# Random-feature attention and a routed expert layer: head reordered, routing cut up, weight pieces regrouped, row buffers freed earlier

## The chip, the cores and the metric

The kernel runs on one core of one Trainium2 chip. The time of a run is the device time of one execution in microseconds (us). The engines are TensorE (PE, its weight loads PEld), VectorE (DVE), ScalarE (ACT), GpSimd (POOL) and SyncE (SP), which only issues transfers. Transfers issued by GpSimd are here the weight pieces, the gathers and the scatters.

## The reference

```python
def _attn_ref(q, k, v, omega):            # q, k, v (8, 8, 576, 64), omega (128, 64)
    def phi(x):
        proj = np.einsum('bhsd,md->bhsm', x, omega)
        return np.concatenate([np.cos(proj), np.sin(proj)], axis=-1) / np.sqrt(m)
    q_p, k_p = (phi(q), phi(k))
    kv = np.einsum('bhsm,bhsd->bhmd', k_p, v)
    z = np.sum(k_p, axis=2)
    num = np.einsum('bhsm,bhmd->bhsd', q_p, kv)
    den = np.einsum('bhsm,bhm->bhs', q_p, z)
    ...
    return num / den
...
x = attn_out.transpose(0, 2, 1, 3).reshape(4608, 512)
def _moe_ref(x, expert_emb, tau, w1, w2): # 8 experts, w1 (8, 512, 1024), w2 (8, 1024, 512)
    xn = x / (np.linalg.norm(x, axis=-1, keepdims=True) + 1e-06)
    en = expert_emb / (np.linalg.norm(expert_emb, axis=-1, keepdims=True) + 1e-06)
    logits = xn @ en.T / tau
    expert_idx = np.argmax(logits, axis=1)
    ...                                   # gate_w: softmax probability of the chosen expert
    for e in range(8):
        mask = expert_idx == e
        h = np.maximum(x[mask] @ w1[e], 0.0)
        out[mask] = gate_w[mask, None] * (h @ w2[e])
```

## The kernel before

The work has three stages. The **head** sets up constants and computes the key side of steps 0 and 1. The **loop** `for n in range(1, NS + 1)` has 32 steps (NS = 32), one for each batch and pair of heads; it is a software pipeline, so step n holds the query side of pair n, the numerator of pair n-1, the key side of pair n+1 and the key projection of pair n+2. The **blocks** `for j in range(NMAIN)` are 40 blocks of 128 tokens, each of one expert; three more stand under a condition.

In a loop step TensorE runs `proj_q` (L245), `num` (L358), `proj_k` (L232), `turns` (L207, L209), `kv_products` (L309) and `kv_turn` (L326 on the products, L333 on the key sums). VectorE runs `frac` (L272) and `fold` (L278), which bring projections into the range of the sine, `split_q` (L201), `kv_copy` (L319) and `norm`. ScalarE rounds (`whole_turns`, L266) and takes sines (`wave`, L284), two for keys and two for queries. GpSimd adds the features over the tokens: `zsum(n, half)` is four additions (L296 to L299) after the sine of that half, and their result `zs` is read by L333. It also issues the weights of the experts as 32 pieces of 512 KB (`emit_weight_piece`, L92 and L98, converted from float32 to float16 on the way): three in the head and one at the end of each step up to 29. On even steps it adds the router's logits (`sums`, L391 to L394).

`set_up_tables`, `set_up_emb`, `set_up_unit` and `set_up_turn` in the head make the router's constants and the matrix `rmat` (L510, GpSimd; L522, VectorE) that `kv_turn` multiplies by. The first three key tiles are copied from PSUM by VectorE (`copy_k`, L218 and L219, tile `w_sb`), later ones by ScalarE.

Routing runs on VectorE in small instructions. `choose_a` (L655 to L658) brings logits together, `choose_b` (L664 to L667) finds the best expert, `choose_c` (L671) marks it, `scan` (L687) counts. `route_first(n)` puts these at steps 9, 10, 17, 18 and 25 to 29, and the placing of the tokens of the first half (`rank`, `places`, `block_hot`, `row_hot`, `rows_of`, `block_experts`) at 18 to 26. In program order a piece of routing stands ahead of `fold(n + 1, "k")` and `frac(n, "q")` on VectorE. `early_second` places the first three quarters of all tokens at steps 30 and 31, and `route_second(j)` the rest in the blocks j = 0 to 7.

In a block, GpSimd issues `gather(j)` (L849, 128 rows of 521 words to a row buffer of `xin_all`), `cast` (L882, to float16), `power` (L893, the norm) and the scatter of the result (L1004). ScalarE squares the rows (L886). VectorE's `score` (L899 to L906) and `weigh` (L916 to L922) work on nine more words of each row, eight logits and the token's number, which `score` reads from the row buffer. TensorE transposes the rows (`turn_x`, L928), and runs `hidden` (L969) and `result` (L991). Gather j+5 uses the buffer of block j or of a block shortly after it, so it waits until the readers of that buffer are through.

The order on every engine is the order in which the program is written; each engine runs its own list, held up only by semaphores.

Of the kernel before, what the change touches and what calls it, by code (L numbers as in the profile page):

```python
# [28 lines left out]
def kernel(  # L29
# [56 lines left out]
    W1BASE, W2BASE = 18046, 83328  # L86

# [50 lines left out]
    with tc.tile_pool(name="psA", bufs=1, space=PSUM) as psA, tc.tile_pool(  # L138
# [150 lines left out]
        def zsum(n, half):  # L289
# [6 lines left out]
            nc.gpsimd.tensor_tensor(zt, t[:, 0:3], t[:, 3:6], ALU.add)  # L296
            nc.gpsimd.tensor_tensor(zt, zt, t[:, 6:9], ALU.add)
# [136 lines left out]
        nc.gpsimd.memset(rmat[64:P, :, :, 0], 0.0)  # L434
        nc.vector.memset(zmask, 0.0)
# [4 lines left out]
        def set_up_tables():  # L440
# [5 lines left out]
            nc.gpsimd.iota(tmpi[:, 0:P], pattern=[[1, P]], base=0, channel_multiplier=0)  # L446
            nc.gpsimd.memset(tri, 0.0)
# [97 lines left out]
        set_up_tables()  # L545
        warm(10)
# [6 lines left out]
        copy_k(0)  # L553
        set_up_norms()
        for b in range(2):
# [8 lines left out]
        turns(1)  # L564
        set_up_emb()
# [172 lines left out]
        def places_a(rk, s0, s1, ar):  # L738
            ns = s1 - s0
            d = [ar.take(ns) for _ in range(4)]  # L740
            pick(d[0], rk[:, :, 0:ns].rearrange("p e s -> p s e"), s0, s1, ar)
            whole(d[1], d[0], -0.49609375)
# [3 lines left out]
            return d  # L746

        def places_b(d, s0, s1, ar):
            shp = [P, s1 - s0, E]
            pick(d[2], bc(sm[:, B1], shp, 1), s0, s1, ar)  # L750
            nc.vector.tensor_tensor(p2["at"][:, s0:s1], d[1], d[2], ALU.add)
            pick(d[3], bc(sm[:, LIM], shp, 1), s0, s1, ar)
            nc.vector.tensor_tensor(p2["ge"][:, s0:s1], d[0], d[3], ALU.is_ge)
# [11 lines left out]
        def places2(w, ge, ns, ar):  # L765
            dest = ar.take(ns)
            lo = ar.take(ns, FP16)
            blk = ar.take(ns, FP16)
# [4 lines left out]
            nc.vector.tensor_reduce(dest.unsqueeze(2), w, axis=AX.X, op=ALU.add)  # L773
            whole(blk, dest, -0.49609375, ar.take(ns))
# [120 lines left out]
        def score(j):  # L895
            t = xin.pop(j).bitcast(FP32)
            s = gsc[:, j % 4]
            rn, mx, sh = s[:, 1:2], s[:, 2:3], s[:, 4 : 4 + E]
            nc.vector.tensor_tensor(  # L899
                ptk[:, j : j + 1], t[:, D + E : D + NG].bitcast(I32), bad[:, j : j + 1], ALU.max  # L900
            )
            lg = t[:, D : D + E]
# [3 lines left out]
            nc.vector.tensor_scalar(sh, lg, mx, rn, ALU.subtract, ALU.mult)  # L906
# [5 lines left out]
        def weigh(j):  # L912
            s = gsc[:, j % 4]
            z = s[:, 3:4]
            sh, dn = s[:, 4 : 4 + E], s[:, 4 + E : 4 + 2 * E]
# [418 lines left out]
```

## Time and profile before

| what | value |
|---|---|
| median of 3 runs | 496.03 us (491.79 to 497.04) |
| the profiled execution | 495.86 us |
| its span, first to last instruction | 494.1 us |
| mean granted clock of TensorE | 0.965 of 2.4 GHz |
| busy, share of the span | PE 93%, POOL 79%, DVE 73%, ACT 69% |

The profiled execution is 0.17 us below the median, and 1.8 us of it lie outside the span. The first loop step begins at 31.90 us, the first `result` of the blocks at 331.53 us, and the last matrix product ends at 484.95 us. A granted clock of 1.00 is 2.4 GHz, 0.50 is 1.2 GHz; a share between them is a mean over the stretch.

### The profile page before, as it was taken

How to read it: one execution, taken by the hardware profiler on the slowest of the kernel's cores; microseconds unless marked ns; L12 is line 12 of the kernel's file. 1: busy time of each engine (PE TensorE's matmuls, PEld its weight loads, DVE VectorE, ACT ScalarE, POOL GpSimd, SP SyncE). 2: the span in 40 equal slices, each digit the busy share in tenths (PEclk: the TensorE clock that was granted, in tenths of full speed). 3: DMA queues.
4: the chain of work that ended last, by engine and by line, in shares of the span. 5: the costliest groups of instructions: out<-in, count | busy, mean ns of one | idle time of the engine just before them, and what ended most of it. 6: DMA issues, size and time to landing. Idle time of an engine off the chain costs nothing. (4 is left out here: it accounts for less than half of the span.)

```text
span 494.1 us, 19396 instructions
## 1 busy us (share of the span) xinstructions
PE 459.2 (93%) x7963; PEld 380.7 (77%) x7963; DVE 360.4 (73%) x969; ACT 338.8 (69%) x475; POOL 388.3 (79%) x519
## 2 busy tenths in 40 slices
PE   8699999989999998998999999699899999999992
PEld 7588887879888887887887888486577777777771
DVE  3747776787766789987889878777876666666671
ACT  2668887978788877887787888357565555555551
POOL 7968898786888787877787888837688888888861
PEclk9779999998999999998999999899899999999997
DMA  6666988887978869889679895506344443443420
GB/s 196 131 146 140 202 169 211 192 172 161 201 166 189 202 141 214 168 199 198 137 187 175 177 222 95 131 24 165 102 131 132 129 133 121 128 134 125 126 74 34
DMA packets 58633, 75.10 MB, mean 152 GB/s; under 512 B 10918, under 2 KB 37542, under 8 KB 58544
## 3 DMA queue, kind: packets, MB, share of 16 engines
q0 software_dynamic: 19200, 35.83, 35.0%
q1 hardware_dynamic: 39040, 37.93, 28.8%
q8 instruction: 65, 1.06, 0.9%
q14 instruction: 24, 0.20, 0.1%
q10 hardware_dynamic: 304, 0.08, 0.1%
HBM read 72.62 MB, written 20.09 MB: 188 GB/s over the span
## 5 line engine op out<-in xcount | busy, mean ns | idle before, releaser
L969 PEld LDWEIGHTS <-w_sb 128*128 x1280 | 74.7, 98 | 10.1 <-issue 1.5
L358 PE MATMUL ps<-kv,siq 128*64 128x73 f32 x1152 | 79.1, 234 | 0.0
L969 PE MATMUL ps<-qr,w_sb 128*128 128x128 f16 x1280 | 78.0, 219 | 0.4 <-DVE qr L197 0.4
L358 PE MATMUL ps<-kv,coq 128*64 128x73 f32 x1152 | 77.3, 231 | 1.0 <-ACT coq L284 1.0
L991 PE MATMUL ps<-w_sb,coq 128*128 x320 | 76.9, 384 | 0.3 <-issue 0.3
L358 PEld LDWEIGHTS ps<-kv,siq 128*64 128x64 f32 x1152 | 60.5, 139 | 12.2 <-issue 11.7
L296 POOL TENSOR_TENSOR zt<-sik 128x384 f32<-128x384 f32 x32 | 43.4, 1355 | 33.6 <-ACT sik L284 33.4
L358 PEld LDWEIGHTS ps<-kv,coq 128*64 128x64 f32 x1152 | 61.4, 141 | 1.2 <-ACT coq L284 1.2
L849 POOL DMA_INDIRECT xin_all<-rf_x,prm x40 | 42.5, 1063 | 23.7 <-issue 13.5
L272 DVE SCALAR_TENSOR_TENSOR cok<-cok,ps 128x1024 f32<-128x1024 f32 (+2 forms) x61 | 46.3, 758 | 16.0 <-ACT cok L266 14.5
L991 PEld LDWEIGHTS <-coq 128*128 128x128 f16 x320 | 30.6, 99 | 29.9 <-issue 2.1
L272 DVE SCALAR_TENSOR_TENSOR coq<-coq,ps 128x1152 f32<-128x1152 f32 x32 | 43.3, 1352 | 12.3 <-ACT coq L266 10.5
L284 ACT ACTIVATE siq<-coq 128x1152 f32<-128x1152 f32 x32 | 37.3, 1164 | 15.2 <-DVE coq L272 9.0
L245 PE MATMUL ps<-qr,omT 32*128 32x288 f32 x512 | 44.4, 432 | 2.9 <-issue 1.7
L886 ACT ACTIVATE qT<-xin_all 128x512 f16<-128x512 f32 x40 | 25.2, 629 | 31.5 <-DMA xin_all<-rf_x,prm 31.5
L284 ACT ACTIVATE cok<-cok,pio 128x1152 f32<-128x1152 f32 x31 | 38.8, 1253 | 10.0 <-DVE cok L278 9.9
L232 PE MATMUL ps<-omT,kT 64*128 64x128 f32 x522 | 41.0, 284 | 4.0 <-DVE coq L272 4.0
L296 POOL TENSOR_TENSOR zt<-cok 128x384 f32<-128x384 f32 x32 | 39.6, 1237 | 5.5 <-ACT cok L284 3.4
L278 DVE TENSOR_SCALAR cok<-cok 128x1152 int32<-128x1152 int32 x31 | 26.5, 854 | 22.0 <-ACT sik L284 21.9
L284 ACT ACTIVATE coq<-coq,pio 128x1152 f32<-128x1152 f32 x32 | 40.2, 1256 | 2.0 <-DVE coq L278 1.9
L232 PEld LDWEIGHTS ps<-omT,kT 64*128 64x128 f32 x522 | 34.8, 187 | 7.0 <-DVE coq L272 4.5
L266 ACT ACTIVATE cok<-ps 128x1152 f32<-128x1152 f32 x31 | 35.0, 1128 | 6.5 <-PE ps L207 4.4
(207 smaller groups left out, 1233.4 us busy)
## 6 DMA issues: line engine op xcount, KB each, us to landing
w_sb<-in_moe_w_dram POOLq DMA_DIRECT2D x32, 512.0 KB, 7.2
qr<-in_q_dram SPq DMA_DIRECT2D x64, 144.0 KB, 5.5
rf_x<-xb SPq DMA_DIRECT2D x32, 288.0 KB, 5.7
kr<-in_k_dram SPq DMA_DIRECT2D x58, 144.0 KB, 4.0
v<-in_v_dram SPq DMA_DIRECT2D x32, 144.0 KB, 4.4
xin_all<-in_v_dram SPq DMA_DIRECT2D x30, 144.0 KB, 8.4
w_sb<-in_k_dram SPq DMA_DIRECT2D x6, 144.0 KB, 2.9
xin_all<-rf_x,prm POOLq DMA_INDIRECT x40, 3.5
```

The lines of the kernel that those rows point to most:

```text
L232: nc.tensor.matmul(kreg[:, KS[c] * P : KS[c] * P + P], lhsT=t[r0 : r0 + 64, j * P : j * P + P], rhs=omT2[r0 : r0 + 64], start=True, stop=True,
L245: nc.tensor.matmul(qreg[:, g // 2, QW * (g % 2) : QW * (g % 2) + QW], lhsT=omT4[r0 : r0 + 32, b], rhs=t[r0 : r0 + 32].rearrange("p (c b j) ...
L266: nc.scalar.activation(dst, src, AF.Copy, bias=CMAGIC, scale=1.0)
L272: nc.vector.scalar_tensor_tensor(out=dst, in0=dst, scalar=CMAGIC, in1=src, op0=ALU.subtract, op1=ALU.subtract)
L278: nc.vector.tensor_scalar(t, t, 0x7FFFFFFF, None, ALU.bitwise_and)
L284: nc.scalar.activation(st[n][which + nm], t, AF.Sin, bias=pio2 if which == "co" else 0.0, scale=-TWO_PI * SINSC,)
L296: nc.gpsimd.tensor_tensor(zt, t[:, 0:3], t[:, 3:6], ALU.add)
L358: nc.tensor.matmul(nm[r0 : r0 + 64, c], lhsT=ph[:, 2 * QW * hh + 64 * c : 2 * QW * hh + 64 * c + 64], rhs=d["kv"][:, hh, half], start=(hal ...
L849: ins = nc.gpsimd.indirect_dma_start(out=t, out_offset=None, in_=x_rows[:], in_offset=bass.IndirectOffsetOnAxis(ap=prm[:, j : j + 1], axis=0),
L886: nc.scalar.activation(late("qT", j % 2, D), xin[j].bitcast(FP32)[:, 0:D], AF.Square, accum_out=gsc[:, j % 4, 0:1],)
L969: nc.tensor.matmul(h_ps[:, f * P : f * P + P], lhsT=weights(k), rhs=d["xT"][:, c * P : c * P + P], start=(c == 0), stop=(c == 3),)
L991: nc.tensor.matmul(y_ps, lhsT=d["hT"][:, c * P : c * P + P], rhs=weights(NW1 + c), start=(c == 0), stop=(c == NW2 - 1),)
```

## The change

Five things change. The pieces of weights are issued two at the very start (ahead of the constant tables on GpSimd), three between the key sums of the head, and then only in odd steps: one between the first and the second addition of `zsum(n + 1, 0)` and one at the step's end. In the head the key side of step 1 comes earlier, `frac(1, "k")` stands ahead of `turns(2)`, and the set-up of the router is spread between. The routing of the first half is spread over more steps in smaller parts, and the third quarter's `choose` moves to steps 27 to 29. In the last steps the gathers 0, 1 and 2 stand at the ends of steps 28, 29 and 30, cast 0 stands ahead of gather 2, and `hot(0)`, `hot(1)` and `hot(2)` (the one-hot tables of places) move into step 32 and into block 0. Finally `cast` gets a second GpSimd instruction, which copies the nine extra words of a row to `gsc`; `score` reads them there, so that the row buffer is read by GpSimd and ScalarE alone.

```diff
+
+    pieces = list(range(4 * E - 4)) + [4 * E - 2, 4 * E - 1, 4 * E - 4, 4 * E - 3]
+
+    def next_piece():
+        if pieces:
+            emit_weight_piece(pieces.pop(0))
...
             nc.gpsimd.tensor_tensor(zt, t[:, 0:3], t[:, 3:6], ALU.add)
+            if between is not None:
+                between()
             nc.gpsimd.tensor_tensor(zt, zt, t[:, 6:9], ALU.add)
             nc.gpsimd.tensor_tensor(z, zt[:, 0], zt[:, 1], ALU.add)
             nc.gpsimd.tensor_tensor(z, z, zt[:, 2], ALU.add)
...
         nc.gpsimd.memset(rmat[64:P, :, :, 0], 0.0)
+        next_piece()
+        next_piece()
...
         proj_q(0)
         load_q(3)
-        turn_emb()
-        set_up_unit()
         for s in cuts:
             part(0, "si", s)
+        copy_k(1)
+        proj_k(1)
+        turn_emb()
+        whole_turns(0, "q")
+        for s in cuts:
             part(0, "fold", s)
-        for s in cuts:
             part(0, "co", s)
         zsum(0, 0)
-        emit_weight_piece(0)
-        copy_k(1)
-        split_q(1)
-        set_up_turn()
-        whole_turns(0, "q")
-        proj_k(1)
+        next_piece()
+        set_up_unit()
+        frac(0, "q")
         whole_turns(1, "k")
-        frac(0, "q")
         kv_products(0)
         zsum(0, 1)
-        emit_weight_piece(1)
+        next_piece()
+        split_q(1)
         wave(0, "si", "q")
+        frac(1, "k", slice(0, P))
+        frac(1, "k", rest)
         turns(2)
-        frac(1, "k")
         wave(1, "si", "k")
+        zsum(1, 0)
+        next_piece()
+        fold(0, "q")
         kv_copy(0)
-        fold(0, "q")
         wave(0, "co", "q")
         load_v(2)
         copy_k(2)
+        set_up_turn()
         fold(1, "k")
         wave(1, "co", "k")
-        zsum(1, 0)
-        emit_weight_piece(2)
+        zsum(1, 1)
         proj_k(2)
-        kv_turn(0)
         turns(3)
         load_k(4)
-        zsum(1, 1)
         whole_turns(2, "k")
         copy_k(3)
+        frac(2, "k", rest)
         kv_products(1)
-        frac(2, "k", rest)
         kv_copy(1)
         frac(2, "k", slice(0, P))
+        kv_turn(0)
...
         def cast(j):
             x16 = late("v", j % 2, D)
             nc.gpsimd.tensor_copy(x16, xin[j].bitcast(FP32)[:, 0:D])
+            nc.gpsimd.tensor_copy(
+                gsc.bitcast(I32)[:, j % 4, 4 : 4 + NG], xin[j][:, D : D + NG]
+            )
             mo[j] = {"x16": x16}
 
         def square(j):
+            t = xin.pop(j).bitcast(FP32)
             nc.scalar.activation(
-                late("qT", j % 2, D), xin[j].bitcast(FP32)[:, 0:D], AF.Square,
-                accum_out=gsc[:, j % 4, 0:1],
+                late("qT", j % 2, D), t[:, 0:D], AF.Square, accum_out=gsc[:, j % 4, 0:1]
             )
 
         def power(j):
@@ -893,17 +917,15 @@
             nc.gpsimd.tensor_tensor(s[:, 1:2], s[:, 0:1], half1, ALU.pow)
 
         def score(j):
-            t = xin.pop(j).bitcast(FP32)
             s = gsc[:, j % 4]
-            rn, mx, sh = s[:, 1:2], s[:, 2:3], s[:, 4 : 4 + E]
+            rn, mx, lg = s[:, 1:2], s[:, 2:3], s[:, 4 : 4 + E]
             nc.vector.tensor_tensor(
-                ptk[:, j : j + 1], t[:, D + E : D + NG].bitcast(I32), bad[:, j : j + 1], ALU.max
-            )
-            lg = t[:, D : D + E]
+                ptk[:, j : j + 1], s.bitcast(I32)[:, 4 + E : 4 + NG], bad[:, j : j + 1], ALU.max
+            )
             nc.vector.tensor_reduce(mx, lg, axis=AX.X, op=ALU.max)
             nc.vector.tensor_scalar(rn, rn, 1e-6, None, ALU.add)
             nc.vector.reciprocal(rn, rn)
-            nc.vector.tensor_scalar(sh, lg, mx, rn, ALU.subtract, ALU.mult)
+            nc.vector.tensor_scalar(lg, lg, mx, rn, ALU.subtract, ALU.mult)
 
         def tanh(j):
             sh = gsc[:, j % 4, 4 : 4 + E]
...
         def route_first(n):
-            if n == 9:
-                choose_a(0)
-                choose_b(0)
-            elif n == 10:
-                choose_c(0)
-                store_logits(0)
-            elif n == 17:
-                choose_a(1)
-                choose_b(1)
-            elif n == 18:
-                choose_c(1)
-                store_logits(1)
-                scan()
-            elif n == 19:
+            if n in (9, 17, 27):
+                choose_a((n - 9) // 8)
+            elif n in (10, 18, 28):
+                choose_b((n - 9) // 8)
+                store_logits((n - 9) // 8)
+            elif n in (11, 19, 29):
+                choose_c((n - 9) // 8)
+                if n > 11:
+                    scan()
+            elif n == 20:
                 r1["rk"] = ar1.take((S1 + 1) * E).rearrange("p (e s) -> p e s", e=E)
                 nc.vector.tensor_copy(r1["rk"], r1["ps"])
-            elif n == 20:
+            elif n == 21:
                 starts1b()
                 r1["wg"] = places(r1["rk"], S1, ar1)
-            elif n == 21:
-                r1["blk"], r1["lo"] = places2(*r1["wg"], S1, ar1)
             elif n == 22:
+                r1["at"] = places2(*r1["wg"], S1, ar1)
+            elif n == 23:
+                r1["blk"], r1["lo"] = places3(r1["at"], S1, ar1)
                 r1["rr"] = block_hot(r1["blk"], S1, 0, K1, ar1)
-            elif n == 23:
+            elif n == 24:
                 row_hot(oh1[:, 0:SG], r1["lo"][:, 0:SG])
-            elif n == 24:
+            elif n == 25:
                 row_hot(oh1[:, SG:S1], r1["lo"][:, SG:S1])
-            elif n == 25:
+            elif n == 26:
                 rows_of(r1["inv"], 0, K1, ar1)
-                choose_a(GRP1)
-            elif n == 26:
                 block_experts(0, K1, False, ar1)
-            elif n == 27:
-                choose_b(GRP1)
-                store_logits(GRP1)
-            elif n == 28:
-                choose_c(GRP1)
-            elif n == 29:
-                scan()
+            elif n == 30:
+                ar = p2["ar"] = Arena(pa.tile([P, 5 * P], FP32, tag="kT", name="ar", bufs=1))
+                p2["lo"] = ar.take(NSLOT, FP16)
+                p2["at"] = ar.take(NSLOT)
+                p2["ge"] = ar.take(NSLOT)
+                p2["d"] = places_a(p2["rk"], 0, S3, ar)
...
@@ -1122,15 +1125,14 @@
                     load_q(n + 3)
             if n == NS:
                 hidden(0, "act")
+                turn_x(1, "dve")
+                hot(0)
                 cast(2)
-                square(2)
-                power(1)
...
-                zsum(n + 1, 0)
+                zsum(n + 1, 0, next_piece if n % 2 else None)
...
-                turn_x(0, "dve")
+                square(0)
...
+            if last:
+                power(0)
+                turn_x(0, "act")
...
-            if n + 2 < NS:
-                emit_weight_piece(n + 2)
+            if n == 29:
+                p2["rk"] = rank(0, S3, ROUTE)
+            if n % 2:
+                next_piece()
             if n == NS - 4:
                 gather(0)
             elif n == NS - 3:
                 gather(1)
+            elif n == NS - 2:
+                places_b(p2["d"], 0, S3, p2["ar"])
+                p2["oh"] = [row_tile(), row_tile()]
+                cast(0)
                 gather(2)
-            elif n == NS - 2:
-                cast(0)
-                square(0)
+            elif last:
+                places_c(p2["d"], 0, S3, p2["ar"])
+                score(0)
                 cast(1)
-            elif last:
-                power(0)
-                score(0)
                 square(1)
                 gather(3)
-                turn_x(1, "dve")
-                early_second(n)
             elif n == NS:
+                power(1)
+                square(2)
                 gather(4)
                 tanh(0)
                 weigh(0)
+                hot(1)
+                score(1)
```

VectorE in step 9 of the loop, before: `choose_a` and `choose_b` stand between `split_q` and the key `fold`.

```order
L201 STREAM_TRANSPOSE qr<-qr 128x576
L655 COPY lsq<-la 64x9x8
L656 COPY lsq<-la 64x9x8
L657 TENSOR_TENSOR lsq<-lsq,la 64x9x8
L658 TENSOR_TENSOR lsq<-lsq,la 64x9x8
L664 TENSOR_REDUCE lmax<-lsq 128x9
L665 TENSOR_TENSOR sel<-lsq,lmax 128x72
L666 TENSOR_TENSOR sel<-sel,pref 128x72
L667 TENSOR_REDUCE pm<-sel 128x9
L278 TENSOR_SCALAR cok<-cok 128x1152
L272 SCALAR_TENSOR_TENSOR coq<-coq,ps 128x1152
```

VectorE in step 9, after: only `choose_a` stands there.

```order
L207 STREAM_TRANSPOSE qr<-qr 128x576
L670 COPY lsq<-la 64x9x8
L671 COPY lsq<-la 64x9x8
L672 TENSOR_TENSOR lsq<-lsq,la 64x9x8
L673 TENSOR_TENSOR lsq<-lsq,la 64x9x8
L284 TENSOR_SCALAR cok<-cok 128x1152
L278 SCALAR_TENSOR_TENSOR coq<-coq,ps 128x1152
```

VectorE in step 10, after.

```order
L207 STREAM_TRANSPOSE qr<-qr 128x576
L679 TENSOR_REDUCE lmax<-lsq 128x9
L680 TENSOR_TENSOR sel<-lsq,lmax 128x72
L681 TENSOR_TENSOR sel<-sel,pref 128x72
L682 TENSOR_REDUCE pm<-sel 128x9
L284 TENSOR_SCALAR cok<-cok 128x1152
L278 SCALAR_TENSOR_TENSOR coq<-coq,ps 128x1152
```

`choose_b` has moved by one step, to the same place between `split_q` and `fold`; `choose_c` follows in step 11.

GpSimd at the end of step 29, before: the last weight piece and two gathers, then the key sums of step 31.

```order
L98 DMA w_sb<-in_moe_w_dram 128x4x512
L849 DMA xin_all<-rf_x,prm 128x521 x2
L296 TENSOR_TENSOR zt<-sik 128x384
L297 TENSOR_TENSOR zt<-zt,sik 128x384
L298 TENSOR_TENSOR zs<-zt 128x128
L299 TENSOR_TENSOR zs<-zs,zt 128x128
```

GpSimd at the same place, after.

```order
L870 DMA xin_all<-rf_x,prm 128x521
L302 TENSOR_TENSOR zt<-sik 128x384
L305 TENSOR_TENSOR zt<-zt,sik 128x384
L306 TENSOR_TENSOR zs<-zt 128x128
L307 TENSOR_TENSOR zs<-zs,zt 128x128
```

The weight piece is gone from here (the last one went at step 27), and gather 2 has moved behind the key sums of step 31.

GpSimd in the blocks, before, one round and the scatter that starts the next.

```order
L1004 DMA out_dram<-siq,ptk 4608x512
L849 DMA xin_all<-rf_x,prm 128x521
L893 TENSOR_TENSOR gsc<-gsc,half_77 128x1
L882 CAST v<-xin_all 128x512
L1004 DMA out_dram<-sik,ptk 4608x512
L849 DMA xin_all<-rf_x,prm 128x521
```

GpSimd in the blocks, after.

```order
L1026 DMA out_dram<-siq,ptk 4608x512
L870 DMA xin_all<-rf_x,prm 128x521
L917 TENSOR_TENSOR gsc<-gsc,half_77 128x1
L903 CAST v<-xin_all 128x512
L904 COPY gsc<-xin_all 128x9
L1026 DMA out_dram<-sik,ptk 4608x512
L870 DMA xin_all<-rf_x,prm 128x521
```

One copy of nine words (L904) has come in behind each cast; the order of the rest is the same. In the program before, such a gather waits for VectorE and for GpSimd; now it waits for GpSimd alone, and the copy waits for VectorE's work on an earlier block's `gsc`.

## Rows read from the trace of the kernel before

**Rows 1.** Windows: engine busy us (instructions), granted clock share, DMA share, GB/s.

```profile
50.00:60.00 10.00, 10.00 (x221) 8.57 (x215) 7.27 (x13) 8.90 (x11) 8.28 (x11) 1.00 0.94 203
310.00:320.00 10.00, 5.10 (x48) 3.90 (x46) 7.18 (x15) 3.63 (x6) 9.42 (x13) 0.82 0.57 139
320.00:330.00 10.00, 8.97 (x187) 8.55 (x184) 7.26 (x16) 4.71 (x9) 2.66 (x3) 0.84 0.04 8
425.00:470.00 45.00, 45.00 (x534) 33.67 (x532) 29.85 (x157) 25.31 (x61) 38.87 (x49) 1.00 0.40 127
```

**Rows 2.** Timeline of TensorE at L245: start, length; steps 2, 9, 10, 11, 29.

```profile
40.84 0.53 PE L245 MATMUL ps<-qr,omT 32*128 32x288 f32 x4
...
103.78 0.53 PE L245 MATMUL ps<-qr,omT 32*128 32x288 f32 x4
...
115.94 0.53 PE L245 MATMUL ps<-qr,omT 32*128 32x288 f32 x4
...
124.69 0.53 PE L245 MATMUL ps<-qr,omT 32*128 32x288 f32 x4
...
295.69 0.53 PE L245 MATMUL ps<-qr,omT 32*128 32x288 f32 x4
```

**Rows 3.** Timeline of VectorE in step 9.

```profile
104.26 0.22 DVE L655 COPY lsq<-la 64x72 f32<-64x72 f32 x1
...
107.70 0.23 DVE L667 TENSOR_REDUCE pm<-sel 128x9 bf16<-128x72 bf16 x1
108.69 1.34 DVE L272 SCALAR_TENSOR_TENSOR coq<-coq,ps 128x1152 f32<-128x1152 f32 x1
```

**Rows 4.** Waits of TensorE, 42 to 300 us: total, times, longest.

```profile
PE ps L232 <- DVE coq L272: 4.0, 3, 1.5
PE ps L245 <- issue: 1.7, 3, 0.7
```

**Rows 5.** Waits of TensorE, 300 to 335 us.

```profile
PE ps L333 <- POOL zs L299: 4.6, 2, 3.8
```

**Rows 6.** Timeline of GpSimd at the end of the loop.

```profile
308.90 1.11 POOL L849 DMA_INDIRECT xin_all<-rf_x,prm  x1 [0.30 <-issue]
310.04 1.02 POOL L296 TENSOR_TENSOR zt<-sik 128x384 f32<-128x384 f32 x1
```

**Rows 7.** Waits of GpSimd, 331 to 370 us.

```profile
POOL xin_all L849 <- DVE gsc L921: 4.6, 3, 3.0
```

**Rows 8.** Waits of TensorE, 331 to 370 us.

```profile
PE ps L928 <- POOL v L882: 2.6, 2, 2.2
```

**Rows 9.** Timeline of GpSimd over one block of the experts.

```profile
426.19 1.04 POOL L849 DMA_INDIRECT xin_all<-rf_x,prm  x1 [0.30 <-DMA xin_all<-rf_x,prm]
427.25 0.58 POOL L893 TENSOR_TENSOR gsc<-gsc,half 128x1 f32<-128x1 f32 x1
427.80 0.61 POOL L882 CAST v<-xin_all 128x512 f16<-128x512 f32 x1
428.58 1.06 POOL L1004 DMA_INDIRECT out_dram<-siq,ptk  x1 [0.18 <-issue]
429.95 1.03 POOL L849 DMA_INDIRECT xin_all<-rf_x,prm  x1 [0.30 <-DMA xin_all<-rf_x,prm]
```

**Rows 10.** Groups of GpSimd by line and shape: busy, mean ns.

```profile
L98 POOL DMA_DIRECT2D w_sb<-in_moe_w_dram x16 | 12.3, 767 | 0.0
...
L510 POOL COPY rmat<-ident 64x128 f32<-64x128 f32 x8 | 2.4, 332 | 0.1
...
L459 POOL IOTA lsq<- 32x16 int32 x4 | 0.7, 163 | 0.1
```

**Rows 11.** Waits of TensorE, 0 to 42 us.

```profile
PE ps L232 <- DVE w_sb L219: 4.5, 3, 2.8
```

**Rows 12.** Timeline of GpSimd in the head.

```profile
33.47 1.51 POOL L296 TENSOR_TENSOR zt<-sik 128x384 f32<-128x384 f32 x1 [3.28 <-ACT sik L284]
```

**Rows 13.** DMA issues by line: count, KB each, median us to landing.

```profile
w_sb<-in_k_dram SPq DMA_DIRECT2D x6, 144.0 KB, 2.9
```

More of the change, by code (lines that the diff above doesn't have):

```diff
@@ L287, in wave, with zsum @@
             )
-        def zsum(n, half):
+        def zsum(n, half, between=None):
             d = st[n]
@@ L438, with set_up_numbers @@
         nc.vector.memset(zmask[64:128, 1:2], 1.0)
-        def set_up_tables():
+        def set_up_numbers():
             for par in range(2):
@@ L446, in set_up_tables @@
             nc.gpsimd.iota(tmpi[:, 0:P], pattern=[[1, P]], base=0, channel_multiplier=0)
+        def set_up_tables():
             nc.gpsimd.memset(tri, 0.0)
@@ L544 @@
         rest = slice(P, NCH * P)
-        set_up_tables()
-        warm(10)
+        warm(5)
         nc.tensor.transpose(tp_om, om2.rearrange("p a d -> p (a d)"), ident)
@@ L553 @@
         copy_k(0)
+        set_up_numbers()
         set_up_norms()
+        set_up_tables()
         for b in range(2):
@@ L564 @@
         turns(1)
+        warm(2)
         set_up_emb()
@@ L741, in places_a, with places_b @@
             pick(d[0], rk[:, :, 0:ns].rearrange("p e s -> p s e"), s0, s1, ar)
+            return d
+        def places_b(d, s0, s1, ar):
+            shp = [P, s1 - s0, E]
             whole(d[1], d[0], -0.49609375)
@@ L745, in places_a, with places_c @@
             )
-            return d
-        def places_b(d, s0, s1, ar):
-            shp = [P, s1 - s0, E]
             pick(d[2], bc(sm[:, B1], shp, 1), s0, s1, ar)
             nc.vector.tensor_tensor(p2["at"][:, s0:s1], d[1], d[2], ALU.add)
+        def places_c(d, s0, s1, ar):
+            shp = [P, s1 - s0, E]
             pick(d[3], bc(sm[:, LIM], shp, 1), s0, s1, ar)
@@ L766, in places2 @@
             dest = ar.take(ns)
-            lo = ar.take(ns, FP16)
-            blk = ar.take(ns, FP16)
             nc.vector.tensor_tensor(w, w, ge, ALU.add)
@@ L773, in places2, with places3 @@
             nc.vector.tensor_reduce(dest.unsqueeze(2), w, axis=AX.X, op=ALU.add)
+            return dest
+        def places3(dest, ns, ar):
+            lo = ar.take(ns, FP16)
+            blk = ar.take(ns, FP16)
             whole(blk, dest, -0.49609375, ar.take(ns))
@@ L1013, in result @@
             tc.add_to_no_dep_group("rows", ins.ins)
-        ar1 = Arena(w2_sb[:, E - 1].rearrange("p c d -> p (c d)").bitcast(FP32))
+        rows_f = xin_all.rearrange("p b w -> p (b w)").bitcast(FP32)
+        ar1 = Arena(rows_f[:, 0:XW], rows_f[:, XW + NCH * 64 :])
         oh1 = (
@@ L1089, in hot @@
             row_hot(p2["oh"][g // 2][:, s : s + SG], p2["lo"][:, SG * g : SG * g + SG])
-        def early_second(n):
-            if n == 30:
-                ar = p2["ar"] = Arena(pa.tile([P, 5 * P], FP32, tag="kT", name="ar", bufs=1))
-                p2["lo"] = ar.take(NSLOT, FP16)
-                p2["at"] = ar.take(NSLOT)
-                p2["ge"] = ar.take(NSLOT)
-                places_b(places_a(p2["rk"], 0, S3, ar), 0, S3, ar)
-                p2["oh"] = [row_tile()]
-                hot(0)
-            elif n == 31:
-                p2["oh"].append(row_tile())
-                hot(1)
-                hot(2)
         nw = n1 + 9
@@ L1124 @@
                 hidden(0, "act")
+                turn_x(1, "dve")
+                hot(0)
                 cast(2)
-                square(2)
-                power(1)
-                score(1)
             if 0 < n < NS:
@@ L1184 @@
             route_pe(n)
-            if not last:
-                early_second(n)
-            early_pe(n)
-            if n + 2 < NS:
-                emit_weight_piece(n + 2)
+            if n == 29:
+                p2["rk"] = rank(0, S3, ROUTE)
+            if n % 2:
+                next_piece()
             if n == NS - 4:
@@ L1209 @@
                 weigh(0)
+                hot(1)
+                score(1)
+        assert not pieces
         r2 = {}
@@ L1231, in route_second @@
                 r2["a"].spare(NSLOT * E)
+                hot(2)
                 choose(NGRP - 1)
@@ L1238, in route_second @@
                 places_b(d, S3, NSLOT, r2["a"])
+                places_c(d, S3, NSLOT, r2["a"])
             elif j == 3:
```

7 lines of the change are left out of this document (3 added, 4 removed).

## The prediction

> **What bounds the kernel now.** I read the windows first. In a stretch of regular loop steps TensorE is busy for 10.00 of 10.00 us at a granted clock of 1.00, and in a stretch of late blocks for 45.00 of 45.00 [rows 1]. So in both stages the matrix products set the pace where nothing disturbs them, and a change can only win where TensorE is short of work, or slow. The timeline of `proj_q` gives the length of a step: from 115.94 to 124.69 it is 8.75. From step 2 (40.84) to step 29 (295.69) there are 27 steps and 254.85 us, where 27 x 8.75 = 236.25 would do: 18.6 us are lost on the way, 3.41 of them in step 9 alone (103.78 to 115.94 is 12.16) [rows 2]. Then come the waits. In the loop TensorE waits 4.0 us in three places for `coq` from VectorE's L272, and 1.7 for nothing that the profile names [rows 4]; at the loop's end 4.6 for the key sums [rows 5], with the clock at 0.82 and 0.84 in the two windows there [rows 1]; in the early blocks GpSimd's gather waits 4.6 for VectorE [rows 7] and TensorE 2.6 for the cast behind it [rows 8]; in the head `proj_k` waits 4.5 for VectorE's key copies [rows 11]. These are what the change touches. The late blocks have a second engine at the limit: GpSimd's round, gather to gather, is 3.76 us of instructions back to back, with only the gaps of 0.30 and 0.18 that stand before every gather and scatter [rows 9]. Whatever is added to that round is added to the time.
>
> **Routing in smaller pieces.** In step 9 `choose_a` and `choose_b` hold VectorE from 104.26 to 107.93, 3.67 us, so that `frac(9, "q")` begins only at 108.69 [rows 3]; the longest wait of TensorE for it is 1.5 [rows 4]. So about 3.67 - 1.5 = 2.2 us of routing fit into a step free of cost, and the rest is paid. The step lost 3.41, not 1.5: after such a wait TensorE ran on at the lower clock (the whole kernel's mean is 0.965). The three waits together cost 4.0 if only the idle time counts, and 4.0 x 3.41 / 1.5 = 9.1 if each costs as step 9 did. I take the middle, 6.5. What comes in: `choose_b` alone at steps 10, 18 and 28. It is at most 3.67 less four instructions of at least 0.22 [rows 3], 2.8, which is 0.6 over the cover, three times 1.8; and `rows_of` with `block_experts` in one step 26, which I leave in the same margin. Forecast -6.5, range -9 to -2.
>
> **Last steps.** Before, two gathers stand ahead of the key sums of step 31; the second starts at 308.90 and the sums at 310.04 [rows 6], so moving it gives them 1.14 + 0.30 of gap = 1.4. The pieces of steps 28 and 29 are gone from there too, so that GpSimd, whose busy share in this window is 9.42 of 10 [rows 1], reaches these sums with no queue behind it. The wait of 4.6 [rows 5] then loses at least 1.4, and at most all of it and the slow products behind it: in 320 to 330 the clock of 0.84 means 3.2 us at 1.2 GHz, and 1.6 us of delay [rows 1]. 4.6 + 1.6 = 6.2. I take the upper end, since two weight pieces of 0.77 [rows 10] and the gather's 1.4 come to 2.9 of the longest wait of 3.8, and its first part, 0.8, goes with them; range -6.5 to -1.4. What is late next is `wave(31, "co", "q")` on ScalarE, which got `square(0)` and the copy of `turn_x(0)` in exchange.
>
> **Early blocks.** The gather of block 5 and those after it wait 4.6 for `weigh` and what stands ahead of it on VectorE, with 3.0 the longest [rows 7]; the change takes this wait away, and nothing hides it, since GpSimd has no spare time in a round [rows 9]. The bounds are the 2.6 that TensorE shows [rows 8] and the 4.6; I take 4.6. Against this, `hot(1)`, `score(1)` and `hot(2)` now stand on VectorE in step 32 and block 0, ahead of the last quarter's routing: the scores and so the scatters come later. The price lies between nothing, if buffers cover it, and those 3.0 of the longest wait. I take 1.
>
> **The copy.** Each round of GpSimd gets L904, nine words by 128. The trace has no such instruction. Below it stands the iota of 16 words, 163 ns; above it the copy of 128 words, 332 ns by its mean [rows 10]. The eight copies are 2.4 us together, 0.30 each, and the cast of 512 words takes 0.61 [rows 9]: the line through these two crosses no words at 0.20. I take 0.18, nearest to the iota. In the 33 blocks behind the routing GpSimd has no cover, so 33 x 0.18 = 6 us. Ends: nothing, if TensorE stays the bound and the copy falls into a gap, and 33 x 0.33 = 11. For the price of so small an instruction the trace thus shows a part that doesn't shrink with size.
>
> The Trainium skill (GPSIMD Engine Reference, 3.1 Elementwise) says otherwise: one-input loops at about 1.8 cycles an element at 1.2 GHz, 769 ns for 512 elements, and in 2.1 only tens of cycles to dispatch an instruction. By that an estimate for nine elements is below 0.1 us, the copies cost under 3, and the sum below would be near 477. The trace's cast is faster than the page's 769 ns, and its small instructions are dearer than the page makes them, so I stay with the rows.
>
> **The head.** TensorE waits 4.5 us in three places for the key copies, 2.8 the longest [rows 11], since copies stood on VectorE behind a `frac` that waited for TensorE. GpSimd, which has all the key sums in its list, idles 3.28 before the sums of step 2 [rows 12]. With key 1 earlier and the `frac` ahead of `turns(2)` the head goes down to what GpSimd's list allows, which makes its idle time the gain, plus what comes from `rmat` moved behind the first sums, under 1. I take -4; bounds 0 and -6. The two pieces issued at the start have nothing to hide them but the loads themselves (a rival, below).
>
> **Weight pieces in odd steps.** GpSimd issues as many; the piece between two additions delays one half of the sums by 0.77 us [rows 10], and the even steps, which carry `sums`, lose theirs. TensorE is full [rows 1] and shows waits for `zs` only at the end of the loop [rows 5], so I cost this at nothing; without the cover it would be 14 odd steps x 0.77 = 11. The unnamed waits, 1.7 for `proj_q` [rows 4] and as many elsewhere, could move either way by 4.
>
> **Sum.** 495.86 - 6.5 - 6.2 - 4.6 + 1 + 6 - 4 = 481.6. The bounds are partly shared: where the copy costs much, the early waits matter less. Half of the 18.6 us lost in the loop lies outside the routing steps, mostly when weights are in flight; fewer pieces late in the loop should take some of this, for which I put 1.6. **Forecast 480 us**; the profiled run and the median of 496.03 are the same for this purpose.
>
> **Rivals.**
> (a) The copy is dear. At 0.33 it costs 11 instead of 6: 485. For it: GpSimd's round has no slack [rows 9]. If it also waits for VectorE's work on `gsc`, a stall like the 3.0 of [rows 7] comes back in its place, 488.
> (b) The early pieces starve the first loads. Key loads of the head land in 2.9 us [rows 13]; with two pieces in flight from the start, the keys of steps 0 and 1 and the values behind them would each be late by up to as much, and the gain of the head is gone: 484. Against it: the first loads are issued before the pieces, from SyncE. The Trainium skill (DMA: Bandwidth & Descriptors, Queues, rings and completion order) has each DMA engine take turns between queue rows, which would halve a load's rate at worst; no row here shows two at the start.
> (c) Slower than before: the piece inside the key sums makes `zs` late in every odd step. TensorE would then wait as it does at the end of the loop. From a delay beyond the slack each 0.77 is paid in full, 11 us, and with the clock falling behind each wait at the rate of step 9 (3.41 for 1.5) it is 25, so 480 + 25 = 505. It decides from the point where GpSimd's list of two steps exceeds 17.5 us; in a regular window it is busy 8.28 of 10 [rows 1], which leaves 3 us in two steps, so I think little of it.
> (d) Better: each routing stall cost as step 9's (-9), the head gives 6, and the copy half as much: 480 - 2.5 - 2 - 3 = 472.5, with the unnamed waits gone too 469. The page's price for the copy alone is inside this case.
>
> **Chances.** Forecast and its neighbourhood (476 to 484) 0.5; (a) 0.15; (b) 0.13; (d) 0.17; (c) 0.05. The range of 8 in 10 reaches from the sum of the better ends, 469, to (a) with its stall and some of (b), 491. A measurement of this kernel can tell about 1% from no change. So: faster by over 1% (below 491) 0.87, within 1% 0.08, slower 0.05.
>
> **What the profile would show.** Right: no wait of `proj_k` on `coq` above 0.5 in steps 9, 17 and 25; `proj_q` of step 2 near 36.8; the wait on `zs` at step 31 under 1; no gather waiting for VectorE; a GpSimd round near 3.93 in the late blocks, with TensorE idle about 0.2 a block. Wrong would be a round still at 3.75 (the copy is free), waits on `zs` in odd steps (c), or the first key load landing late (b). The largest doubt is the size of the copy, 33 times.

## The result: 477.2 us, ratio 0.966, and where the time went

| | before | changed |
|---|---|---|
| median of 4 runs, us | 493.91 (490.94 to 497.04) | 477.22 (476.70 to 477.97) |
| ratio to before | | 0.9663, 95% interval 0.9589 to 0.9736 |
| span of the profiled execution, us | 494.1 | 476.1 |

Cut at marks that both profiles have, the 18.0 us of the span lie here (`r0`, `r8` and `r38` are the first products of `result` in these blocks; before they stand at 331.53, 368.30 and 481.33):

| stretch | before | changed | difference | forecast |
|---|---|---|---|---|
| start to `proj_q` of step 2 | 40.84 | 39.33 | -1.5 | -4 |
| step 2 to step 29 | 254.85 | 237.79 | -17.1 | -6.5 and -1.6 |
| step 29 to `r0` | 35.84 | 30.04 | -5.8 | -6.2 |
| `r0` to `r8` | 36.77 | 38.09 | +1.3 | -4.6 + 1 |
| `r8` to `r38` | 113.03 | 118.42 | +5.4 | +6 |
| `r38` to the end | 12.73 | 12.42 | -0.3 | 0 |

The marks in the timeline of TensorE, changed kernel (start, length); the first two answer to [rows 2].

```profile
39.33 0.53 PE L251 MATMUL ps<-qr,omT 32*128 32x288 f32 x4
...
277.12 0.77 PE L251 MATMUL ps<-qr,omT 32*128 32x288 f32 x8
...
307.16 1.03 PE L1013 MATMUL ps<-w_sb,coq 128*128 x4
...
345.25 0.59 PE L1013 MATMUL ps<-w_sb,coq 128*128 x2
...
463.67 0.59 PE L1013 MATMUL ps<-w_sb,coq 128*128 x2
```

Waits of TensorE from 42 to 300 us, changed kernel, all that there are. Against [rows 4] and [rows 5] the waits for `coq` in front of `proj_k` and the unnamed ones in the loop are gone; what is left stands between 285 and 297, at the loop's end.

```profile
PE ps L341 <- POOL zs L307: 0.8, 1, 0.8
PE ps L334 <- issue: 0.7, 1, 0.7
PE ps L317 <- DVE coq L278: 0.2, 1, 0.2
```

One round of GpSimd in a late block, changed kernel, beside [rows 9]: 418.46 to 422.40 is 3.94, and the copy is what has been added.

```profile
418.46 1.04 POOL L870 DMA_INDIRECT xin_all<-rf_x,prm  x1 [0.30 <-issue]
419.53 0.58 POOL L917 TENSOR_TENSOR gsc<-gsc,half 128x1 f32<-128x1 f32 x1
420.08 0.60 POOL L903 CAST v<-xin_all 128x512 f16<-128x512 f32 x1
420.64 0.23 POOL L904 COPY gsc<-xin_all 128x9 int32<-128x9 int32 x1
421.04 1.05 POOL L1026 DMA_INDIRECT out_dram<-sik,ptk  x1 [0.17 <-issue]
422.40 1.05 POOL L870 DMA_INDIRECT xin_all<-rf_x,prm  x1 [0.31 <-issue]
```

The three longest waits of TensorE in the head (0 to 42 us) of the changed kernel, beside [rows 11]: the wait for VectorE's copies has shrunk from 4.5 to 1.1, and one for a key load is new.

```profile
PE ps L213 <- DMA w_sb<-in_k_dram: 1.5, 1, 1.5
PE ps L512 <- POOL half L440: 1.4, 1, 1.4
PE ps L238 <- DVE w_sb L225: 1.1, 2, 0.8
```

The key loads there, beside [rows 13]:

```profile
w_sb<-in_k_dram SPq DMA_DIRECT2D x6, 144.0 KB, 6.5
```

### The profile page after: what moved, and what is told of

Its sections match the earlier page's. It is cut to its first block, busy times and chain, and to the rows that moved or that the text cites. A ratio compares the mean times of both kernels' runs of the same rounds, so it can differ in the third digit from the quotient of the medians.

```text
span 476.1 us, 19438 instructions
## 1 busy us (share of the span) xinstructions
PE 451.0 (95%) x7957; PEld 371.6 (78%) x7957; DVE 357.3 (75%) x969; ACT 337.1 (71%) x476; POOL 395.9 (83%) x559
## 5 line engine op out<-in xcount | busy, mean ns | idle before, releaser
L366 PE MATMUL ps<-kv,siq 128*64 128x73 f32 x1152 | 76.4, 229 | 0.0
L1013 PE MATMUL ps<-w_sb,coq 128*128 x320 | 75.4, 378 | 0.1
L366 PE MATMUL ps<-kv,coq 128*64 128x73 f32 x1152 | 74.9, 226 | 0.0
L366 PEld LDWEIGHTS ps<-kv,siq 128*64 128x64 f32 x1152 | 58.5, 135 | 11.7 <-issue 11.2
L366 PEld LDWEIGHTS ps<-kv,coq 128*64 128x64 f32 x1152 | 59.6, 137 | 0.0
L278 DVE SCALAR_TENSOR_TENSOR cok<-cok,ps 128x128 f32<-128x128 f32 (+1 forms) x62 | 46.3, 748 | 13.1 <-ACT cok L272 13.1
L290 ACT ACTIVATE siq<-coq 128x1152 f32<-128x1152 f32 x32 | 37.3, 1164 | 10.2 <-DVE coq L278 8.8
L251 PE MATMUL ps<-qr,omT 32*128 32x288 f32 x512 | 41.3, 436 | 0.0
L307 POOL TENSOR_TENSOR zs<-zs,zt 128x128 f32<-128x128 f32 x64 | 36.7, 573 | 5.0
L272 ACT ACTIVATE coq<-ps 128x1152 f32<-128x1152 f32 x32 | 36.0, 1125 | 5.3 <-PE ps L238 4.7
L302 POOL TENSOR_TENSOR zt<-cok 128x384 f32<-128x384 f32 x32 | 37.3, 1164 | 2.5
```

Source lines behind the costliest of these rows:

```text
L251: nc.tensor.matmul(qreg[:, g // 2, QW * (g % 2) : QW * (g % 2) + QW], lhsT=omT4[r0 : r0 + 32, b], rhs=t[r0 : r0 + 32].rearrange("p (c b j) ...
L272: nc.scalar.activation(dst, src, AF.Copy, bias=CMAGIC, scale=1.0)
L278: nc.vector.scalar_tensor_tensor(out=dst, in0=dst, scalar=CMAGIC, in1=src, op0=ALU.subtract, op1=ALU.subtract)
L290: nc.scalar.activation(st[n][which + nm], t, AF.Sin, bias=pio2 if which == "co" else 0.0, scale=-TWO_PI * SINSC,)
L307: nc.gpsimd.tensor_tensor(z, z, zt[:, 2], ALU.add)
L366: nc.tensor.matmul(nm[r0 : r0 + 64, c], lhsT=ph[:, 2 * QW * hh + 64 * c : 2 * QW * hh + 64 * c + 64], rhs=d["kv"][:, hh, half], start=(hal ...
```

## The experiments

Three groups of four, in the order of the table, each group on one chip; the result above comes from a fourth. Chips differ: before took 505.6, 508.8 and 495.3 us on the three, so a median counts only beside its own group, and stretches from the traces carry most of the argument. The first group has no run of the unaltered changed kernel. The loop can be compared across chips: step 2 to 29 of the changed program took 237.79, 237.87 and 237.80 on the result's chip and on those of the second and third group.

| kernel | ratio to before (95%) | to step 2 | 2 to 29 | 29 to `r0` | `r0` to `r8` | `r8` to `r38` |
|---|---|---|---|---|---|---|
| one_piece | 0.987 (0.979 to 0.995) | 36.02 | 246.29 | 31.29 | 38.30 | 132.67 |
| even_pieces | 1.002 (0.996 to 1.009) | 39.89 | 251.01 | 29.40 | 38.07 | 132.67 |
| old_routing | 0.998 (0.994 to 1.001) | 39.54 | 248.09 | 30.34 | 38.17 | 132.75 |
| no_copy | 0.967 (0.960 to 0.974) | 39.29 | 237.79 | 31.69 | 44.17 | 124.55 |
| control | 0.974 (0.964 to 0.983) | 39.15 | 237.87 | 30.30 | 38.19 | 131.78 |
| no_early | 0.970 (0.960 to 0.979) | 36.44 | 238.46 | 30.88 | 38.12 | 131.89 |
| before_odd_pieces | 0.985 (0.981 to 0.990) | 42.19 | 247.98 | 36.43 | 38.88 | 123.20 |
| copy_to_12 | 0.973 (0.964 to 0.982) | 40.28 | 238.17 | 30.02 | 38.08 | 131.75 |
| control_b | 0.969 (0.960 to 0.977) | 40.03 | 237.80 | 30.06 | 38.04 | 118.04 |
| no_copy_b | 0.961 (0.953 to 0.969) | 39.40 | 237.81 | 30.06 | 39.00 | 113.14 |
| mix_a | 0.960 (0.952 to 0.968) | 36.34 | 238.24 | 33.29 | 37.91 | 113.76 |
| mix_b | 0.959 (0.952 to 0.966) | 37.22 | 237.88 | 32.69 | 38.62 | 113.11 |

**Weight pieces: one_piece, even_pieces, before_odd_pieces.**

```diff
 # one_piece (in the changed kernel); the two calls at the start go as well
-                zsum(n + 1, 0, next_piece if n % 2 else None)
+                zsum(n + 1, 0)
-            if n % 2:
+            if n + 2 < NS:
                 next_piece()
 # even_pieces (in the changed kernel), at both places
-                zsum(n + 1, 0, next_piece if n % 2 else None)
+                zsum(n + 1, 0, next_piece if n % 2 == 0 else None)
-            if n % 2:
+            if n % 2 == 0:
                 next_piece()
 # before_odd_pieces (in the kernel before)
-                zsum(n + 1, 0)
+                zsum(n + 1, 0, next_piece if n % 2 else None)
-            if n + 2 < NS:
-                emit_weight_piece(n + 2)
+            if n % 2 and n < 28:
+                next_piece()
```

> The changed kernel (477.2 us) with the weight pieces put back as before: none at the start, three between the key sums of the head, one at the end of every step up to 29. Theory A (the unnamed waits of TensorE in the loop come from a piece of weights in flight together with the row stores of an even step, which makes TensorE's own instruction loads late): steps such as 6, 12, 14, 16 and 21 lose 1 to 2 us again, with waits put down to nothing, 7 to 10 us in all, and the pieces of steps 28 and 29 delay the last key sums by 1 to 2: 485 to 489. Theory B (as predicted: regrouping the pieces is worth little, the gain of the loop is the routing): 477 to 480.

> The changed kernel with the pieces of the loop issued two in every even step, instead of two in every odd step. Theory A (row stores and pieces collide): both pieces now go with the row stores, so the unnamed waits are as large as before or larger: 485 to 492. Rival C (it is enough that pieces come in pairs with a free step between): 477 to 479. Theory B: 477 to 479 as well.

> The kernel before with one edit: the pieces of the loop come two in every odd step, the first of them inside the key sums (three in the head as before). Theory A (pieces together with row stores make TensorE's instruction loads late): the unnamed waits in steps 6, 12, 14, 16 and 21 go, the waits for routing stay, steps 2 to 29 take 245 to 249 us in place of 254.9, and the kernel is 6 to 9 us faster than before. Rival D (the unnamed waits are a consequence of the routing stalls and of the head's phase): steps 2 to 29 stay above 252, and less than 3 us are gained.

Waits of TensorE from 40 to 300 us of one_piece, of even_pieces, and from 42 to 292 of before_odd_pieces:

```profile
PE ps L317 <- issue: 3.9, 2, 2.3
PE ps L251 <- issue: 1.7, 2, 1.5
PE ps L317 <- DVE coq L278: 0.2, 1, 0.2
```

```profile
PE ps L251 <- issue: 2.5, 4, 0.9
PE ps L317 <- issue: 2.4, 1, 2.4
PE ps L238 <- DVE coq L278: 1.9, 1, 1.9
```

```profile
PE ps L232 <- DVE coq L272: 7.3, 4, 2.1
```

The waits put down to "issue" (the engine waited for nothing that the profile names) are there with one piece a step and with pieces in even steps, and absent with pieces in odd steps, in the changed program and in the one before. The loop is 8.5 us longer with one piece a step than as changed (246.29 - 237.79) and 13.2 longer with even steps; in the kernel before, the odd steps alone save 6.9 (254.85 - 247.98). Of the 13.2, 3.7 stand in step 9 behind the wait of 1.9 for VectorE, which is of another kind (see the routing below). The effect that theory A foretold is there, and B, C and D are ruled out. In one_piece the places were not those expected: the loss is in steps 16, 18 and 27 to 29, not 6, 12 and 14.

The DMA view of one_piece shows what is late (q0 carries GpSimd's transfers, q1 those of SyncE, q8 instructions). First its queues from 257.6 to 266.4 us, with no row for the instruction queue, then from 266.4 to 269, with one load of instructions (16 KB):

```profile
q1 hardware_dynamic: 1418, 1.02, 46.8%
q0 software_dynamic: 444, 0.45, 42.3%
```

```profile
q1 hardware_dynamic: 264, 0.48, 73.3%
q0 software_dynamic: 84, 0.08, 18.5%
q8 instruction: 1, 0.02, 2.5%
```

And TensorE there, which runs dry in the middle of `kv_products` and goes on behind that load:

```profile
266.18 0.27 PE L317 MATMUL ps<-cok,v 64*64 64x128 f32 x1
268.75 0.32 PE L317 MATMUL ps<-cok,v 64*64 64x128 f32 x1 [2.31 <-issue]
```

For 8.8 us row stores, loads and weights take the 16 DMA engines to a share of 0.89 with no instruction load among them. In the changed kernel 43 such loads start between 40 and 290 us, never more than 8.1 apart; in the kernel before 40, up to 10.0 apart. In the steps 2 to 29 of the kernel before, one_piece and even_pieces there are 13 waits of 0.3 us or more put down to "issue", and each of them ends 1.2 to 1.7 us after such a load has ended. That the late load is what TensorE waited for follows from this order in time; no run changed that load alone. Why it is late stays open: a full set of DMA engines is not enough, since their share is 0.92 from 42 to 277 us in the changed kernel, which has no such wait, and no run tried the row stores apart from whatever else an even step does.

**Routing: old_routing.**

```diff
-            if n in (9, 17, 27):
+            if n in (9, 17):
                 choose_a((n - 9) // 8)
-            elif n in (10, 18, 28):
                 choose_b((n - 9) // 8)
+            elif n in (10, 18):
+                choose_c((n - 9) // 8)
...
```

> The changed kernel with the routing of the first three quarters of the tokens at the steps of before (9, 10, 17 to 29), the rest as changed. As predicted, the three long pieces in steps 9, 17 and 25 make TensorE wait again for 1.0 to 1.5 us each and run slow behind it: 4 to 9 us more, 481 to 486. Rival: with the pieces of weights out of the way VectorE and the loads run ahead, and the same routing costs under 2: 477 to 479.

Its longest waits of TensorE from 40 to 300 us:

```profile
PE ps L238 <- DVE coq L278: 7.2, 4, 2.1
```

The loop is 10.3 us longer. The same four waits, 7.3 in all, are in before_odd_pieces: with the pieces in odd steps the routing stalls are larger than the 4.0 in three places of [rows 4]. The rival is refuted, and the range expected (4 to 9) was too low.

The traces show more than a long piece of work. VectorE and GpSimd in step 9 of the kernel before, inside the 3.67 us of [rows 3]:

```profile
105.86 0.78 DVE L665 TENSOR_TENSOR sel<-lsq,lmax 128x72 bf16<-128x72 f32 x1
106.67 1.00 DVE L666 TENSOR_TENSOR sel<-sel,pref 128x72 bf16<-128x72 bf16 x1
```

```profile
105.52 1.01 POOL L296 TENSOR_TENSOR zt<-sik 128x384 f32<-128x384 f32 x1
106.61 1.00 POOL L297 TENSOR_TENSOR zt<-zt,sik 128x384 f32<-128x384 f32 x1
```

The same two instructions of VectorE take 0.23 and 0.20 in step 27 of the same trace. Here each lasts until GpSimd's addition beside it is through, which makes 1.35 of the 3.67. In before_odd_pieces and old_routing, where a weight piece stands between the two additions, the second lasts 1.68 and 1.66, and the wait of TensorE in this step grows from 1.5 to 2.1. In the changed kernel `choose_a` and `choose_b` stand clear of the additions in steps 9, 10, 17 and 18 and take 0.20 to 0.23 an instruction of this kind. A small piece alone is no cure: in even_pieces step 9 has only `choose_a`, but the weight piece of step 8 moves the additions beside it, its two `TENSOR_TENSOR` last 1.53 and 1.04, TensorE waits 1.9, and the step is 3.7 us longer. So it counts where a piece of routing falls beside the key sums, and not its length alone. That GpSimd holds VectorE is read from these times; no run took the sums away.

**The copy: no_copy, copy_to_12, no_copy_b.** In no_copy gather 4 stood ahead of the scores of block 1, which so read the rows of block 4; its early blocks count for nothing, its late ones do. no_copy_b puts that right.

```diff
 # no_copy, no_copy_b (copy_to_12: under "if j < 13 or j >= NMAIN")
-            nc.gpsimd.tensor_copy(
-                gsc.bitcast(I32)[:, j % 4, 4 : 4 + NG], xin[j][:, D : D + NG]
-            )
 # no_copy_b
                 square(2)
+                score(1)
                 gather(4)
...
-                score(1)
```

> The changed kernel without the nine-word copy on GpSimd: the scores read the row buffer again, and the gathers wait for VectorE. If the copy costs its 0.21 us in each late block, blocks take 3.74 again in place of 3.93, 5 to 6 us less over the late blocks, and the early blocks lose up to 4.6 to gathers that wait for VectorE: 471 to 476. If the copy is hidden and the early release is worth much: 478 to 482.

> The changed kernel with the nine-word copy only in blocks 0 to 12; later scores read the row buffer. As the copy costs 0.2 us of each late round, blocks 13 and later take 3.74 instead of 3.93: 5 us less than the control. Rival: on a chip where the round falls into its longer form of 4.45 us anyway, the copy matters little, under 3 us.

> The changed kernel without the copy, with the scores of block 1 put ahead of gather 4 so that they read the right rows. If the copy is what pushes the blocks out of the short round, blocks 10 to 20 take 3.74 as before; against the control blocks 8 to 38 are 5 to 8 us shorter, the early ones up to 4.6 longer for gathers that wait for VectorE: 1 to 6 us faster in all. Rival (the long round comes from the chip alone): no difference above 2.

On the chip of the third group no_copy_b took 474.03 us (473.98 to 476.67) beside 478.64 (477.19 to 479.60) of control_b: 4.6 less. From `r8` to `r38` it gains 4.9, near the 30 x 0.18 = 5.4 of the forecast's price; from `r0` to `r8` it loses 1.0. On the chip of the first group the late blocks of no_copy are 8.1 to 8.2 shorter than those of its three neighbours (124.55 against 132.67 to 132.75): the copy is dearer there, since without it the longer round told in the last section begins later. The waits of GpSimd in the early blocks (307 to 345 us), of the changed kernel and of no_copy_b:

```profile
POOL out_dram L1026 <- ACT siq L1025: 3.9, 2, 2.6
POOL la L402 <- DVE gsc L938: 3.6, 1, 3.6
POOL out_dram L1026 <- ACT sik L1025: 2.7, 2, 1.4
```

```profile
POOL xin_all L870 <- DVE gsc L948: 5.6, 3, 3.2
POOL xin_all L870 <- DVE gsc L943: 1.4, 2, 1.0
```

The release by GpSimd does remove the gathers' waits of [rows 7], but scatters that wait for results take their place. copy_to_12 gave nothing on its chip (131.75 against 131.78 of control from `r8` to `r38`), as its rival said.

**Controls, the early pieces, mixtures: control, no_early, control_b, mix_a, mix_b.**

```diff
 # no_early, mix_a, mix_b
-        next_piece()
-        next_piece()
         nc.vector.memset(zmask, 0.0)
 # mix_a, mix_b: hot(2) from j == 0 to j == 1; copy for j < 8 (mix_a) or none (mix_b, with score(1) as in no_copy_b)
 # mix_b
-            if j == 20:
+            if j == 36:
                 nbv = nc.values_load(
```

> The changed kernel unaltered, on the chip of the three runs beside it, since chips differ (before took 494 us on the first chip and 506 on the second): the ratio to before should be 0.96 to 0.98, with steps of the loop as in its first profile (step 2 at 39.3 us, step 29 at 277.1).

> The changed kernel without the two pieces of weights at the very start (the rest of the list moves up, the last pieces come in step 29). If these pieces held up the first key loads, step 2 begins near 36.0 instead of 39.3, as in the run with one piece a step, and the kernel is 2.5 to 3.5 us faster than the control. If the head is bound by GpSimd's list whatever the loads do, step 2 stays at 38 to 39.5.

> The changed kernel unaltered, beside the three runs that follow: ratio to before 0.965 to 0.975; late blocks 3.93 or 4.45 us each, according to the chip, from block 11 on.

> The changed kernel with three edits: no pieces at the very start, the third one-hot table built in block 1 and not ahead of the last quarter's routing in block 0, and the copy in blocks 0 to 7 only. Expected from the parts: head -2.7, TensorE's wait for the routing in block 1 (2.3 us) down by the table's 1.3, blocks 10 to 20 at 3.74: 6 to 11 us faster than the control. If the long round of late blocks is entered because of blocks 8 to 12 and not of the copy, only 3 to 4 are gained.

> As the run before, but with no copy at all, and with the read of the block count, which all engines do at block 20, at block 36. If this read is what tips blocks 22 and later into the round of 4.45 in kernels without the copy, these blocks stay at 3.74 and the kernel is the fastest of all, 8 to 15 us under the control. If not, blocks 22 and later look as without this edit.

Without the early pieces step 2 begins 2.7 us earlier (36.44 against 39.15), and the six key loads of [rows 13] land in 3.0 us in place of the control's 7.6, so the pieces did hold up the keys. But 0.6 is lost again in the loop, mostly in steps 2 and 3, and 0.6 between step 29, where the list of pieces now ends, and `r0`. The medians differ by only 1.7 us (490.41 against 492.08), less than the spread of either. In mix_a the gain is lost entirely: step 29 is 3.3 earlier than in control_b and `r0` at the same time. TensorE waits 2.4 for the last key sums (280 to 309 us), where control_b waits 1.0, and behind that wait its granted clock is 0.50 from 296 to 300 us, where control_b keeps 1.00 from 293 to `r0`:

```profile
PE ps L341 <- POOL zs L307: 2.4, 1, 2.4
```

Moving the table shortened block 1 by 1.5 us (6.58 to 5.08) and lengthened block 2 by 1.5 (4.26 to 5.79): the order of VectorE's routing gave nothing here, and that its sum is the bound is argued, not shown. mix_a and mix_b came 4.4 and 4.5 us under control_b (474.25 and 474.10), where 6 to 11 and 8 to 15 had been expected; they are as fast as no_copy_b, which is the simplest of the kernels that beat the changed one, and their late blocks gained what its did. On a chip without the long round mix_b can't show what it was made for.

## Why the prediction was right, point by point

The time (477.2 against 480, range 469 to 491) and the sign held, but in good part by luck. The loop gained 9.0 us more than its two terms (17.1 against 8.1), the head and the early blocks together 7.4 less than theirs, and the two nearly cancel.

- **Routing** (-6.5, range -9 to -2): right in kind, too small. With the pieces as before it measures 8.6 in the loop (254.85 - 246.29 of one_piece), near the 9.1 that counts the slow clock behind each wait; in step 9 of the kernel before the granted clock is 1.00 up to the wait of 1.5 and 0.50 from 112 to 114 us. With the pieces in odd steps it measures 10.2 to 10.3 (247.98 - 237.79 of before_odd_pieces, and old_routing): the piece between two additions makes the stalls longer and adds a fourth, of 1.5 to 1.6 in step 21, which the kernel before doesn't have. The step that was incomplete is the length of the piece: 3.67 was taken as VectorE's own work, but 1.35 of it was spent beside GpSimd's additions. By an estimate from the same rows 2.3 are left without that, about the 2.2 that the prediction found free of cost.
- **Weight pieces** (at nothing, with 1.6 for the unnamed waits): the step that failed most. Regrouping them is worth 6.9 in the kernel before and 8.5 in the changed one. I had seen half of the 18.6 us lost in the loop outside the routing steps and left it at "could move either way by 4". The gains of the loop add up in either order: 8.6 + 8.5 or 6.9 + 10.2 make the 17.1.
- **Last steps** (-6.2): -5.8. The wait for `zs` fell from 4.6 to 0.8. Which of the edits did it is not shown: before_odd_pieces has no pieces behind step 27, its wait for `zs` is 2.4, and its stretch from step 29 to `r0` is no shorter (36.43 against 35.84).
- **Early blocks** (-4.6 + 1): +1.3. The gathers' wait went as said, but the release itself is worth 1.0 (no_copy_b), not 4.6: the step that failed is "nothing hides it". The price of the tables moved there was taken too low as well: TensorE waits 2.3 for the scan of the last quarter (0.2 before), behind two one-hot tables of 1.34 each. mix_a, with one of the two moved on, waits 1.0 there and gains nothing over the blocks.
- **The copy** (+6): +5.4, the copy 0.21 on average in 40, the round 3.94 where 3.93 was forecast. An estimate from the Trainium skill (GPSIMD Engine Reference, 3.1 Elementwise) had put it below 0.1 us; the trace's 0.21 decides for the rows. One sign failed: TensorE shows no idle time of 0.2 a block, but is recorded busy for 40.00 of 40.00 us from 425 to 465. So a full TensorE, as in [rows 1], did not show that it sets the pace of the late blocks.
- **The head** (-4): -1.5. The reorder gives 4.4 (40.84 - 36.44 of no_early, on different chips), and the early pieces take 2.7 (no_early) to 3.7 (mix_a against control_b) of it back: rival (b), to two thirds or more. Step 2 began at 39.33, not near 36.8, and the key loads landed in 6.5 us where 2.9 stood in [rows 13], more than twice as long, where (b) took a halved rate for the worst.
- **Rival (c)**: no wait for `zs` in an odd step up to 29; the piece between two additions costs nothing in the changed kernel, though it lengthens the stalls of the old routing.

Wait of the routing in block 1, changed kernel, waits of TensorE from 315 us on:

```profile
PE ps L707 <- DVE cumx L702: 2.3, 1, 2.3
```

## What to carry to other kernels

Waits that a profile puts down to nothing are worth a look at the DMA queue that carries instructions: here TensorE ran dry before late instruction loads when weights were issued in the steps that also store rows, and moving them by one step cost or saved 7 to 9 us. When a short instruction of VectorE shows several times its usual length, see what GpSimd does beside it before cutting the work up. Before adding even 0.2 us to an engine whose round equals the bound, multiply by the number of rounds; an early release that is needed in eight blocks should not be paid in forty. Work moved out of one full stretch must be priced in the stretch that takes it in.

## What the runs showed of the hardware

As the order in time has it, an engine's list is held up here by more than semaphores: by the late instruction loads of one_piece, and on VectorE by GpSimd. Over the first 300 us of nine traces (before, after, one_piece, even_pieces, old_routing, before_odd_pieces, control, no_early, control_b) the `TENSOR_TENSOR` instructions of `choose_a` and `choose_b` take 0.20 to 0.25 us 84 times and 0.37 to 1.74 us 24 times, and each of the 24 runs beside an addition of GpSimd.

On two of the chips the same program has a longer round in the late blocks: 4.3 to 4.6 us a block from block 11 on where there is a copy in blocks 8 to 12 (control, copy_to_12), and from block 22 or 23 on without any (no_copy, before_odd_pieces). With the copy, the time from `r8` to `r38` is then 131.75 to 132.75 us in place of 118. On the chip of the third group no run of four showed it. Timeline of control, TensorE, VectorE and ScalarE in one such block:

```profile
443.19 0.39 PE L950 MATMUL ps<-ident,v 128*128 128x128 f16 x4
443.41 1.89 PE L1013 MATMUL ps<-w_sb,coq 128*128 x8
444.85 0.69 DVE L1003 TENSOR_SCALAR coq<-ps 128x512 f16<-128x512 f32 x1 [1.85 <-PE ps L950]
445.34 0.69 ACT L1025 ACTIVATE sik<-ps,gpos 128x512 f32<-128x512 f32 x1 [1.48 <-PE ps L1013]
445.46 0.41 DVE L203 COPY qr<-ps 128x512 f16<-128x512 f16 x1
445.93 0.27 PE L991 MATMUL ps<-qr,w_sb 128*128 128x128 f16 x2 [0.63 <-DVE qr L203]
```

VectorE's half of `hidden` starts at 444.85 after 1.85 us of idle time, which the profile puts down to the transposes of L950; TensorE's records, whose ends are modelled, have these done by 443.58, 1.27 earlier. Everything behind it shifts. Why VectorE is released so late there, and only on some chips, is open: no run took apart the read of the next expert's number that stands on TensorE at this place, and the copy's absence in late blocks (copy_to_12) doesn't end it once it has begun.
